# Moving the last tokens' product of blocks 2 to 5 beside the product with q, into the banks of w_res and of w_out's first product

## The chip, the cores and the metric

The kernel runs on one core of a Trainium2 chip. The metric is the device time of one execution in microseconds (us); lower is better. It is written with an order laid down by hand: nothing reorders the instructions of an engine, and each engine works through its own list in order. The engines are TensorE (PE in the profile, with its weight loads as PEld), VectorE (DVE), ScalarE (ACT), GpSimd (POOL), and the queue of SyncE (SP) for transfers.

## The reference

Attention without softmax, then a gated feed-forward part with a gated residual. Batch 8, 8 heads, 576 tokens, head size 64; so x has 4608 rows of 512, and d_ff is 1536.

```
kv  = einsum('bhsd,bhse->bhde', k, v)
out = einsum('bhsd,bhde->bhse', q, kv)
rms = sqrt(mean(out * out, axis=-1) + 1e-06)
x   = (out / rms * g_norm), heads side by side: 4608 x 512

g, val   = x @ w_gate, x @ w_val
ffn_out  = (gelu(g) * val) @ w_out
res_gate = sigmoid(x @ w_res)
result   = x + res_gate * ffn_out
```

## The kernel before, in words

**Blocks.** The first 512 tokens of batch b are block b (0 to 7). The last 64 tokens of all eight batches are gathered into block 8, two batches to a tile of 128 rows. While block m goes through the feed-forward part, the attention of batch b = m+2 is done in between. For b = 4 to 7 (blocks m = 2 to 5) this includes the last 64 tokens of a pair of batches, 2(b-4) and 2(b-4)+1, whose q lies transposed in `qrT`.

**Seven products in place of eight.** Each large product is cut in quadrants and done by Winograd's scheme with seven products of half size. A block's gate and value products run in three groups of four columns of 128 (`gv_group`, line 952). The group's order is a string of words (lines 946 to 950): `1g` is the first product of the gate, `Eg` a ScalarE copy that seeds a second PSUM bank, `Fg` and `cg` are VectorE sums, `g11` is a gelu on ScalarE, `h11` the product gelu x value. A block's last group ends `... 3g cv 3v h11 g22 4g g12 h12 4v g21 h22 h21`. Other work is hung behind a word with `at_word`, and is issued right after it.

**Banks.** PSUM has eight banks. A tile is given a bank by number, and its first writer waits until all that used the bank's former tile are done. `banks_of` (line 1522) hands a group's banks on by role. In a last group the gate's tiles A, E, F are in the banks called `ga1`, `gf`, `ge_` there, the value's in `va1`, `vf`, `ve`, and `ga0`, `va0` are free. `out_at` gives the banks of what follows, `att_at` and `pattn.opening` those of the attention's tiles.

**Behind the groups.** `res_halves` (line 577) makes the product with w_res in tiles rA, rF, rE, again by words: `1` and `6` write rA, `5` rF, `2` rE; `sE` is the ScalarE copy of rA into rE, `sd` that of rF into `rd`, `+F` the VectorE sum of rA and rd; `7` writes rA again. In blocks 2 to 5 `with_res_and_attn` (line 678) hangs attention and the first products of w_out (tiles wA, wD, wE, wF) between these words; behind `sd` it puts `a_o`, q times kv, 32 small matmuls into four tiles named op.

**The last tokens before the change.** `a_rem_kv` (line 274) takes two banks. `rem_mm` (line 282) multiplies the last tokens' q with kv: 16 matmuls of 64x64x64 for the chip's four quarters of the array, into one half of kv's own bank (kvp) and into a second bank (orp). `kv_mm` makes kv itself, 40 small matmuls, in the other half of the first bank. For b = 4 to 6 both stand behind `3g` in the block's last group; for b = 7, which needs its own kv for its last tokens, kv stands behind `5v` and `rem_mm` behind `3g`. `kv_out` (line 294) casts kv to `kv2` on ScalarE, and `rem_out` (line 297) copies the two outputs to `o32`, behind the word `g12` (for b = 7 the cast is behind `dv`). `s_begin` (line 519) is a VectorE difference of 128x1536 hidden values, hung behind `h12`.

Of the kernel before, what the change touches and what calls it, by code (L numbers as in the profile page):

```python
# [8 lines left out]
FP32 = mybir.dt.float32  # L9
# [9 lines left out]
def kernel(  # L19
# [204 lines left out]
                    )  # L224

    def a_kv(b, copy=nc.vector.tensor_copy):
        ps = pattn.tile([P, NP, D], FP32, tag="at", name="kvp")
        kv_mm(b, ps)
        copy(out=st[b]["kv2"], in_=ps)

    def a_o(b):

# [38 lines left out]
        a_sq(b, i)  # L271
        a_red(b, i)

    def a_rem_kv(b):

        kv = pattn.tile([P, 2, NP, D], FP32, tag="at", name="kvp")
        st[b]["ps"] = kv[:, 1], [kv[:, 0], pattn.tile([P, NP, D], FP32, tag="at", name="orp")]
        if 2 * pair(b) + 1 < b:
            rem_mm(b)
        kv_mm(b, kv[:, 1])  # L280

    def rem_mm(b):
        for pr in range(NP):
            for e in range(2):
                for i in range(2):
                    nc.tensor.matmul(
                        st[b]["ps"][1][e][halves(i), pr, :],
                        lhsT=st[b]["qrT"][halves(e), pr, halves(i)],
                        rhs=kv_of(2 * pair(b) + i, e, pr),
                        start=True,  # L290
                        stop=True,
                    )

    def kv_out(b):
        nc.scalar.copy(out=st[b]["kv2"], in_=st[b]["ps"][0])  # L295

    def rem_out(b):
        o32 = attnp.tile([P, C], FP32, tag="o32", bufs=3, name="o32")
        st[b]["o"][NJ] = o32
        for e in range(2):  # L300
            nc.scalar.copy(
                out=o32.rearrange("p (r e d) -> p r e d", e=2, d=D)[:, :, e, :], in_=st[b]["ps"][1][e]
            )

    def a_norm(b, j0, j1, eng=nc.vector):
# [333 lines left out]
    def out_by_products(blk, banks, amid):  # L639
# [38 lines left out]
        def with_res_and_attn():  # L678
            b = blk + 2

            def tile_of_w(n):
                w[n] = pmoe.tile([P, 2, CH], FP32, name="w" + n, bank=banks[n])

            def half_a(e):
                if e == 0:
                    tile_of_w("A")
                half("A", e, a_of(blk, 1, 1), b_of(1, 1))

            def seed():
                tile_of_w("E")  # L690
                nc.scalar.copy(out=w["E"], in_=w["A"])

            def behind_a():
                tile_of_w("F")
                tile_of_w("D")
                for e in range(2):
                    half_d(e)
                for i in (2, 3):
                    a_ss(b, i)
                w["d"] = attnp.tile([P, 2, CH], FP32, tag="sq", bufs=3, name="wd")  # L700
                nc.scalar.copy(out=w["d"], in_=w["D"])

            res_halves(blk, dict(zip("AFE", (banks[j] for j in range(3)))), {
                "sE": [lambda: sq_tile(b, 0), lambda: sq_tile(b, 1)],
                "sd": [lambda: s_sum(blk, 0), lambda: a_o(b), lambda: a_sq(b, 0), lambda: a_sq(b, 1)],
                "+F": [lambda: a_red(b, 0)],
                "2": [lambda: half_a(0)],
                "tE": [lambda: a_sq(b, NJ)],
                "+c": [lambda: s_sum(blk, 1), lambda: a_red(b, 1), lambda: a_red(b, NJ)],
                "3": [lambda: half_a(1)],  # L710
                "tF": [seed],
                "tA": [behind_a],
            }, "1 sE 5 sd 6 +F 2 tE 7 +c 3 tF 4 tA tc")
            for jj in ((0, 0), (0, 1), (1, 1), (1, 0)):
                sigmoid(jj)
# [721 lines left out]
    def plan_attn_ahead(b):  # L1437

        rem = pair(b) is not None
        m = b - 2  # L1440
        assert rem == (m in GROUPS)
        act, pool = nc.scalar.copy, nc.gpsimd
        begin = [lambda: attn_begin(b), lambda: d_qT(b)]
        if rem:
            at_word(m, 0, "h22", begin.pop(0), lambda: d_rem_qT(b))
        if m in GROUPS:
            for i in range(2):
                half = lambda i=i: by_token(b, act, slice(2 * i, 2 * i + 2))
                if whole(m):
                    at_word(m, i, "g11", half)  # L1450
                else:
                    at(m, 2 + i, half)
            if whole(m):
                at_word(m, 1, "g11", *begin)
            else:
                at(m, 3, *begin)
            if b + 1 < B:
                at(m, 2 * GF, lambda: load_behind(b))
            last = len(GROUPS[m]) - 1
        else:  # L1460
            at(m, 8, lambda: by_token(b, act, slice(0, 2)))
            at(m, 9, lambda: by_token(b, act, slice(2, 4)), *begin)
            at(m, NF, lambda: a_kv(b, act), lambda: load_behind(b, load_q))
            aside_out(m, "end", lambda: load_kv(b + 1))
        if rem:
            at_word(m + 2, 0, "cv", lambda: a_g(b, NJ, NJ + 1))
            own = 2 * pair(b) + 1 == b
            at_word(m, last, "5v" if own else "3g", lambda: a_rem_kv(b))
            at_word(m, last, "dv" if own else "g12", lambda: kv_out(b))
            if own:  # L1470
                at_word(m, last, "3g", lambda: rem_mm(b))
            at_word(m, last, "g12", lambda: rem_out(b))
        else:
            at(m, NF + 1, lambda: a_o(b), *[lambda j=j: a_ss(b, j) for j in range(NJ)])
        aside_out(m, "F", lambda: a_norm(b, 0, NJ + rem, pool))
        first = [lambda: new_block(b), lambda: a_t(b, 0), lambda: a_t(b, 1)]
        if whole(m + 1):
            aside_out(m, "01" if m + 1 == WHOLE else "11", *first[0:2])
            upper = [] if m + 1 == WHOLE else [lambda: d_xT(b, 0, 2)]
            amid_out[m].setdefault("end", [])[0:0] = [first[2], *upper]  # L1480
        else:
            at(m, NF + 3, *first)
        if whole(m + 1):
            t = [lambda j=j: a_t(b, j) for j in range(NJ)]
            if rem:
                at_word(m + 1, 0, "h21", lambda: a_t(b, NJ), lambda: d_xT(b, NJ, NJ + 1))
            first_whole = m + 1 == WHOLE
            for i, word, fs in (
                (0, "Fv", t[2:3]),
                (0, "cv", [t[3], lambda: d_xT(b, 0 if first_whole else 2, NJ)]),  # L1490
                (2 if first_whole else 1, "Fv" if first_whole else "cv", [lambda: a_g(b, 0, 2)]),
                (2, "Fv", [lambda: a_g(b, 2, NJ)]),
            ):
                at_word(m + 1, i, word, *fs)
            return
        for j in range(2, NJ + rem):
            at(m + 1, j - 2, lambda j=j: a_t(b, j))
        at(m + 1, 1, lambda: d_xT(b, 0, NJ))
        at_word(m + 1, 1, "Fv", lambda: a_g(b, 0, 2))
        at_word(m + 1, 1, "cv", lambda: a_g(b, 2, NJ))  # L1500
# [21 lines left out]
    def banks_of(blk):  # L1522
# [18 lines left out]
        if blk not in LAST:  # L1541
            if len(groups) % 2:
                ga0, ga1, va0, va1, ge_, gf, ve, vf = ga1, ga0, va1, va0, gf, ge_, vf, ve
            out_at[blk] = {0: ge_, 1: ve, 2: ga1, "A": va1, "D": ga1, "E": ve, "F": ge_}
            att_at[blk] = [gf, vf, ga0, va0]
            if res_in_halves(blk):
                out_at[blk] = {0: ga0, 1: va0, 2: ve, "A": gf, "D": vf, "E": ge_, "F": ga1}
                att_at[blk] = [ga0, va0, ve, va1]
            pmoe.turn = [out_at[blk][n] for n in "DEFA"]
        else:  # L1550
            out_at[blk] = {0: ga1, 1: va1, 2: ge_, 3: ve}
            if blk == LAST[0]:
                out_at[blk].update(A=gf, D=vf, E=ga0, F=va0)
            else:
                out_at[blk].update(A=(gf, vf), D=ga0, E=va0, F=ga1)
# [5 lines left out]
    for blk in range(B + 1):  # L1561
# [21 lines left out]
        else:  # L1583
            slots = [lambda f=f: m_gval(blk, f) for f in range(NF)]
            groups = GROUPS.get(blk, ())
            if groups:
# [1 line left out]
                slots[n:] = [None] * (NF - n)  # L1588
                ends = []
                if not res_in_halves(blk):  # L1590
                    at_word(blk, len(groups) - 1, "h12", lambda: s_begin(blk))

                def group(i, blk=blk, ends=ends):
                    if i == 0:
                        ends.extend(banks_of(blk))
                        if blk + 2 < B:
                            o = att_at[blk]
                            pattn.opening = o[2:] + o
                    order = None if i == 0 and whole(blk) else i == len(GROUPS[blk]) - 1
                    gv_group(blk, GROUPS[blk][i], ends[i], amid_gv.get((blk, i), {}), order)  # L1600

# [90 lines left out]
```

## Time and profile before

| what | time |
|---|---|
| median of 3 runs (318.71 to 319.44) | 319.14 us |
| profiled execution | 318.52 us |
| its span | 316.5 us |
| TensorE busy | 308.2 us, 97% of the span |
| VectorE busy | 275.7 us, 87% |
| ScalarE busy | 217.0 us, 69% |
| GpSimd busy | 187.4 us, 59% |

Block 2 ends at about 121 us, block 3 at 154, block 4 at 187 and block 5 at 219. In the views, a row of the timeline has start, duration, engine, line, operation, output and input, and in brackets how long the engine was idle before it and what released it. Rows of TensorE overlap: a matmul of 128x256 is issued each 0.109 us and its result is there 0.27 us after it starts, so "x4, 0.60" is 0.44 us of TensorE and then the time for the last result to arrive. ScalarE's and VectorE's rows overlap a little too; the distance from start to start is what a row costs in a queue.

### The profile page before, as it was taken

The numbers are of one execution on the slowest core, as the hardware profiler recorded it, in microseconds if no ns is written. First come the engines' busy times: TensorE is split into PE (matmuls) and PEld (weight loads), VectorE is DVE, ScalarE is ACT, GpSimd is POOL, SyncE is SP. The second block draws the span as 40 slices with busy tenths as digits, with TensorE's granted clock in tenths as the row PEclk, the third lists the DMA queues.
The fourth block names the chain that finished last, engine by engine and source line by source line (L and its number), as shares of the span: only waits on it lengthen the run. The fifth ranks groups of instructions, "written<-read, shape, count | busy, mean of one in ns | idle before, by whom it ended". The sixth has DMA issues, their size and how long they took to land.

```text
span 316.5 us, 7841 instructions
## 1 busy us (share of the span) xinstructions
PE 308.2 (97%) x3071; PEld 249.1 (79%) x3071; DVE 275.7 (87%) x489; ACT 217.0 (69%) x395; POOL 187.4 (59%) x239
## 2 busy tenths in 40 slices
PE   7899999999999999999999999999999999999993
PEld 3555756844888888888888888888888888888882
DVE  5897998989898899989998999899998777897774
ACT  4764688685958794879487948795667367736760
POOL 2883352360799579856985798408850474396332
PEclk9999999999999999999999999999999999999997
DMA  7999999899969598389936994700630003001104
GB/s 253 330 201 204 200 198 197 154 171 209 121 78 177 180 158 110 72 198 150 116 67 201 128 124 71 217 4 0 78 142 1 2 5 131 0 2 59 76 2 133
DMA packets 77398, 38.91 MB, mean 123 GB/s; under 512 B 42290, under 2 KB 75058, under 8 KB 77362
## 3 DMA queue, kind: packets, MB, share of 16 engines
q0 software_dynamic: 39296, 17.17, 43.3%
q1 hardware_dynamic: 37488, 20.71, 26.1%
q8 instruction: 24, 0.39, 0.5%
q10 hardware_dynamic: 578, 0.52, 0.5%
q14 instruction: 12, 0.10, 0.1%
HBM read 38.80 MB, written 9.44 MB: 152 GB/s over the span
## 4 chain that ended last, share of the span: by engine, by line
PE 59%; DVE 1%; issue 0%; DVEq 0%
PE Av L981 10%; PE Ag L981 10%; PE wA L549 8%; PE Fv L981 5%; PE Fg L981 5%; PE rA L600 3%; PE w L549 2%; PE Eg L981 2%; PE Ev L981 2%; PE wF L549 2%; PE wE L549 2%; PE wD L549 2%; PE rF L600 2%; PE rE L600 1%; PE kvp L218 1%; PE op L240 1%
## 5 line engine op out<-in xcount | busy, mean ns | idle before, releaser
L1018 POOL TENSOR_TENSOR hid<-ge,c 128x512 f16<-128x512 f16 x23 | 26.8, 1165 | 36.5 <-ACT ge L1012 36.5
L549 PEld LDWEIGHTS <-hid_s 128*128 128x128 f16 x384 | 37.5, 98 | 4.5
L981 PEld LDWEIGHTS <-wsv 128*128 128x128 f16 x368 | 35.6, 98 | 4.8 <-issue 0.2
L981 PEld LDWEIGHTS <-wsg 128*128 128x128 f16 x368 | 35.8, 98 | 4.2
L394 POOL TENSOR_TENSOR t<-t,g 128x512 f16<-128x512 f16 x32 | 37.8, 1210 | 0.0
L737 POOL TENSOR_TENSOR osb<-osb,t 128x512 f32<-128x512 f32 x28 | 34.0, 1244 | 0.0
L991 ACT COPY Eg<-Ag 128x512 f32<-128x512 f32 x23 | 13.4, 582 | 26.2 <-PE Ag L981 25.6
L549 PEld LDWEIGHTS <-hid 128*128 128x128 f16 x288 | 28.1, 98 | 3.3
L981 PEld LDWEIGHTS <-wg 128*128 128x128 f16 x276 | 27.0, 98 | 3.6
L981 PEld LDWEIGHTS <-wv 128*128 128x128 f16 x276 | 27.0, 98 | 3.1
L981 PE MATMUL Ag<-ts,wsg 128*128 128x256 f16 x184 | 27.6, 273 | 0.0
L981 PE MATMUL Av<-ts,wsv 128*128 128x256 f16 x184 | 27.6, 272 | 0.0
L1002 DVE TENSOR_TENSOR Fg<-Ag,d 128x512 f32<-128x512 f32 x23 | 16.0, 696 | 12.0 <-ACT d L995 9.1
L268 DVE TENSOR_REDUCE ss<-sq 128x8 f32<-128x512 f32 x32 | 20.3, 677 | 0.6 <-ACT sq L263 0.5
L549 PE MATMUL wA<-wo_ts,hid_s 128*128 128x256 f16 x168 | 20.6, 272 | 0.0
L1012 ACT ACTIVATE ge<-Eg 128x512 f16<-128x512 f32 x23 | 13.7, 597 | 9.7 <-PE Eg L981 9.7
L1012 ACT ACTIVATE ge<-c 128x512 f16<-128x512 f32 x23 | 14.4, 625 | 8.0 <-DVE c L1002 8.0
L1012 ACT ACTIVATE ge<-Fg 128x512 f16<-128x512 f32 x23 | 13.6, 591 | 8.8 <-PE Fg L981 7.0
L1002 DVE TENSOR_TENSOR c<-Ag,d 128x512 f32<-128x512 f32 x23 | 15.8, 688 | 4.2 <-PE Ag L981 4.2
L377 DVE TENSOR_TENSOR t<-op,ny 128x512 f16<-128x512 f32 x28 | 18.7, 683 | 0.9 <-POOL ny L334 0.4
L1018 DVE TENSOR_TENSOR hid<-ge,Fv 128x512 f16<-128x512 f16 x23 | 15.6, 680 | 1.5 <-ACT kv L295 1.5
L1012 ACT ACTIVATE ge<-Ag 128x512 f16<-128x512 f32 x23 | 13.7, 598 | 4.1 <-PE Ag L981 4.0
(228 smaller groups left out, 857.1 us busy)
## 6 DMA issues: line engine op xcount, KB each, us to landing
out_dram<-osb SPq DMA_DIRECT2D x14, 512.0 KB, 3.6
qraw<-in_q_dram POOLq DMA_DIRECT2D x7, 512.0 KB, 6.4
k<-in_k_dram POOLq DMA_DIRECT2D x7, 512.0 KB, 7.9
v<-in_v_dram POOLq DMA_DIRECT2D x7, 512.0 KB, 10.7
wo<-in_moe_w_out_dram POOLq DMA_DIRECT2D x3, 384.0 KB, 11.9
wg<-in_moe_w_gate_dram POOLq DMA_DIRECT2D x2, 512.0 KB, 8.4
out_dram<-osb SPq DMA_DIRECT2D x4, 256.0 KB, 5.0
wv<-in_moe_w_val_dram POOLq DMA_DIRECT2D x3, 256.0 KB, 7.5
```

The costliest lines, as they stand in the source:

```text
L218: nc.tensor.matmul(ps[halves(e), pr, :], lhsT=k16[:, h, j * D : (j + 1) * D] if j < NJ else kl[:, h, :], rhs=v16[:, h, j * D : (j + 1) * D ...
L268: nc.vector.tensor_reduce(out=out_, in_=sqs.pop((b, i)), op=ALU.add, axis=mybir.AxisListType.X)
L377: nc.vector.tensor_tensor(out=t, in0=o, in1=scale, op=ALU.mult)
L394: eng.tensor_tensor(out=t_t[blk][:, jj, :], in0=t_t[blk][:, jj, :], in1=g16, op=ALU.mult)
L549: nc.tensor.matmul(ps[:, e - es[0], :], lhsT=a[:, f, e * P : (e + 1) * P], rhs=b[:, f, :], start=(start and e == es[0] and f == 0), stop=( ...
L600: nc.tensor.matmul(out_[:, e, :], lhsT=x_[:, e, cc, :], rhs=w_[:, cc, :], start=(first and e == 0 and cc == 0), stop=(cc == 1), skip_group ...
L737: nc.gpsimd.tensor_tensor(out=res_all[of], in0=res_all[of], in1=t_t[blk][of], op=ALU.add)
L981: nc.tensor.matmul(out_[:, r, :], lhsT=lhsT, rhs=rhs, start=(first and r == 0 and c == 0), stop=(c == 1), skip_group_check=True,)
L991: nc.scalar.copy(out=tile_of("E", u), in_=ps["A", u])
L1002: nc.vector.tensor_tensor(out=dst, in0=ps["A", u], in1=sb["d", u], op=ALU.add)
L1012: nc.scalar.activation(out=ge[q], in_=source(q, "g"), func=AF.Gelu)
L1018: eng.tensor_tensor(out=dst, in0=ge[q], in1=source(q, "v"), op=ALU.mult)
```

## The change

In blocks 2 to 5 the 16 matmuls of the last tokens leave the group. They are now issued behind the first product with w_res (word `1`), followed by `a_o`, which moves there from behind `sd`, and by the two ScalarE copies, which leave `g12`. So TensorE's order is rA's first product, the 16 matmuls, op, rF; ScalarE's is the gelu of Ag, the two copies, rA to rE, rF to rd.

The 16 matmuls write two banks of their own: that of rF (the last group's Fv) and that of wA (the last group's Ag). wA and wD exchange banks, and rE goes from Ag's bank to Av's. kv has its bank alone, and takes one bank ahead of the op tiles in place of two. The VectorE difference `s_begin` moves from behind `h12` to behind `h21`, which puts it after the product of gelu with Av. Blocks 0, 1, 6, 7 and 8 have the same instructions in the same order as before, and no instruction of POOL or SP moves.

```diff
-    def a_rem_kv(b):
-        kv = pattn.tile([P, 2, NP, D], FP32, tag="at", name="kvp")
-        st[b]["ps"] = kv[:, 1], [kv[:, 0], pattn.tile([P, NP, D], FP32, tag="at", name="orp")]
-        if 2 * pair(b) + 1 < b:
-            rem_mm(b)
-        kv_mm(b, kv[:, 1])
+    def a_kv_mm(b):
+        st[b]["kvp"] = pattn.tile([P, NP, D], FP32, tag="at", name="kvp")
+        kv_mm(b, st[b]["kvp"])
+
+    def a_kv_out(b, copy=nc.scalar.copy):
+        copy(out=st[b]["kv2"], in_=st[b]["kvp"])
...
-    def rem_mm(b):
+    def a_rem(b, banks):
+        st[b]["orp"] = [pmoe.tile([P, NP, D], FP32, name="orp", bank=n) for n in banks]
         for pr in range(NP):
             for e in range(2):
                 for i in range(2):
                     nc.tensor.matmul(
-                        st[b]["ps"][1][e][halves(i), pr, :],
+                        st[b]["orp"][e][halves(i), pr, :],
...
             res_halves(blk, dict(zip("AFE", (banks[j] for j in range(3)))), {
+                "1": [lambda: a_rem(b, (banks[1], banks["A"])), lambda: a_o(b), lambda: rem_out(b)],
                 "sE": [lambda: sq_tile(b, 0), lambda: sq_tile(b, 1)],
-                "sd": [lambda: s_sum(blk, 0), lambda: a_o(b), lambda: a_sq(b, 0), lambda: a_sq(b, 1)],
+                "sd": [lambda: s_sum(blk, 0), lambda: a_sq(b, 0), lambda: a_sq(b, 1)],
...
-            at_word(m, last, "5v" if own else "3g", lambda: a_rem_kv(b))
-            at_word(m, last, "dv" if own else "g12", lambda: kv_out(b))
-            if own:
-                at_word(m, last, "3g", lambda: rem_mm(b))
-            at_word(m, last, "g12", lambda: rem_out(b))
+            at_word(m, last, "5v" if own else "3g", lambda: a_kv_mm(b))
+            at_word(m, last, "dv" if own else "g12", lambda: a_kv_out(b))
...
-            out_at[blk] = {0: ge_, 1: ve, 2: ga1, "A": va1, "D": ga1, "E": ve, "F": ge_}
+            out_at[blk] = {0: ge_, 1: ve, 2: va1, "A": ga1, "D": va1, "E": ve, "F": ge_}
...
-                    at_word(blk, len(groups) - 1, "h12", lambda: s_begin(blk))
+                    at_word(blk, len(groups) - 1, "h21", lambda: s_begin(blk))
...
-                            pattn.opening = o[2:] + o
+                            pattn.opening = o[2:3] + o
```

More of the change, by code (lines that the diff above doesn't have):

```diff
@@ L226, in a_kv @@
     def a_kv(b, copy=nc.vector.tensor_copy):
-        ps = pattn.tile([P, NP, D], FP32, tag="at", name="kvp")
-        kv_mm(b, ps)
-        copy(out=st[b]["kv2"], in_=ps)
+        a_kv_mm(b)
+        a_kv_out(b, copy)
+    def a_kv_mm(b):
[3 more added lines that the diff above has]
+        copy(out=st[b]["kv2"], in_=st[b]["kvp"])
     def a_o(b):
@@ L292, in rem_mm @@
                     )
-    def kv_out(b):
-        nc.scalar.copy(out=st[b]["kv2"], in_=st[b]["ps"][0])
     def rem_out(b):
@@ L301, in rem_out @@
             nc.scalar.copy(
-                out=o32.rearrange("p (r e d) -> p r e d", e=2, d=D)[:, :, e, :], in_=st[b]["ps"][1][e]
+                out=o32.rearrange("p (r e d) -> p r e d", e=2, d=D)[:, :, e, :], in_=st[b]["orp"][e]
             )
```

## The prediction

> **What bounds the kernel now.** I read the page's busy times first, then the table of busy time by stretch, then the timeline of block 3, and last the rows around the same place in blocks 2, 4 and 5.
>
> ```profile
> PE 308.2 (97%) x3071; PEld 249.1 (79%) x3071; DVE 275.7 (87%) x489; ACT 217.0 (69%) x395; POOL 187.4 (59%) x239
> ...
> core 0: us, PE busy (x) PEld busy (x) DVE busy (x) ACT busy (x) POOL busy (x), PEclk, DMA share, GB/s
> ...
> 186.60:219.30 32.70, 32.70 (x371) 28.60 (x369) 30.57 (x50) 24.56 (x46) 18.38 (x25) 1.00 0.34 75
> ```
>
> TensorE is the bound, and in the blocks that the change touches it is never idle: in block 5 (186.60 to 219.30) it is busy for all 32.70 us, at full clock. Between 86 and 219 us the list of waits has no wait of TensorE for another engine. So the change can't win by removing a wait of TensorE here. It can win only TensorE time, and it loses wherever it puts a wait in front of TensorE. Here is block 3 from the end of its last group into the seven products with w_res:
>
> ```profile
> 138.81 0.22 PE L286 MATMUL orp<-kv,qrT 64*64 64x64 f16 x2
> ...
> 138.93 0.20 PE L286 MATMUL orp<-kv,qrT 64*64 64x64 f16 x2
> ...
> 139.05 0.32 PE L218 MATMUL kvp<-v,k 128*64 128x64 f16 x8
> ...
> 139.81 0.61 PE L981 MATMUL Fv<-xT,wsv 128*128 128x256 f16 x4
> 139.92 0.37 ACT L295 CAST kv<-kvp 128x256 f16<-128x256 f32 x1
> ...
> 140.19 0.38 ACT L301 COPY o<-kvp 128x256 f32<-128x256 f32 x1
> 140.25 0.60 PE L981 MATMUL Ag<-ts,wg 128*128 128x256 f16 x4
> 140.45 0.39 ACT L301 COPY o<-orp 128x256 f32<-128x256 f32 x1
> 140.51 0.69 DVE L1018 TENSOR_TENSOR hid<-ge,Fv 128x512 f16<-128x512 f16 x1 [0.59 <-ACT kv L295]
> ...
> 140.89 0.60 ACT L1012 ACTIVATE ge<-Ag 128x512 f16<-128x512 f32 x1
> ...
> 141.12 0.95 DVE L512 TENSOR_TENSOR hid_s<-hid 128x1536 f16<-128x1536 f16 x1
> 141.13 0.60 PE L600 MATMUL rA<-wr,xT 128*128 128x256 f16 x4
> ...
> 141.56 0.60 PE L600 MATMUL rF<-wrs,ts 128*128 128x256 f16 x4
> 141.82 0.57 ACT L620 COPY rE<-rA 128x512 f32<-128x512 f32 x1 [0.33 <-PE rA L600]
> 141.99 0.68 DVE L1018 TENSOR_TENSOR hid<-ge,Av 128x512 f16<-128x512 f16 x1
> ...
> 142.10 0.64 PE L240 MATMUL op<-kv,qT 64*128 64x64 f16 x32
> ...
> 142.58 0.95 DVE L512 TENSOR_TENSOR hid_s<-hid 128x1536 f16<-128x1536 f16 x1
> 142.67 0.61 PE L600 MATMUL rA<-wrs,ts 128*128 128x256 f16 x4
> ...
> 143.45 0.69 DVE L627 TENSOR_TENSOR rF<-rA,rd 128x512 f32<-128x512 f32 x1
> ...
> 144.21 0.60 PE L600 MATMUL rA<-wrs,ts 128*128 128x256 f16 x4
> ```
>
> See how little is to spare. I count from the start of rA's first product, R (141.13). ScalarE copies rA into rE (141.82 to 142.39) while TensorE does rF and op, and the next product into rA (142.67, R+1.54) finds the copy done 0.28 us earlier. The seventh product (144.21, R+3.08) follows the end of VectorE's rF sum (143.45+0.69=144.14) by 0.07 us. Blocks 2 and 4 have the same offsets (R is 108.54 and 173.55, the next rA product 110.08 and 175.09).
>
> **The change, part by part, blocks 2 to 4.**
>
> *What leaves the group.* The last tokens' 16 matmuls take 0.24 us of TensorE (138.81 to 139.05, the change of array shape included). kvp and everything up to rA come 0.24 us earlier, so rA starts at R-0.24. Two ScalarE copies leave the place ahead of the gelu of Ag; kv's cast stays.
>
> *May the product start in its new place?* Its two outputs lie in the banks of Fv and Ag. The reader of Ag is that gelu: Ag's matmuls end at 140.25+0.60-0.24=140.61, the gelu starts 0.04 later (as 140.85 to 140.89 now) and ends at R+0.12. Fv's reader on VectorE starts at 140.27 and ends at R-0.17. A product of small tiles begins 0.54 after the start of the product ahead (141.56 to 142.10), thus at R+0.30. A release reaches TensorE 0.05 to 0.09 us after the releaser's end (0.07 in the rows above, 209.25 to 209.30 in block 5, 44.35 to 44.44 from the cast of batch 1's kv to its op). So there is no wait, with about 0.1 us to spare.
>
> *What is now behind it on ScalarE.* This is the step that costs. On ScalarE the order is: both copies of the result, then the copy rA to rE, then rd. Last matmul at R+0.30+0.12, its result 0.20 later (138.81, 138.93, 0.20): R+0.62. The first copy starts 0.04 (gelu row) to 0.09 later (rA ends at 141.73, the copy starts at 141.82). The next starts 0.25 to 0.27 after it (205.48 to 205.73 in block 5; 140.19 to 140.45), and rA to rE 0.25 to 0.29 after that (205.73 to 205.99; 108.02 to 108.31 in block 2): R+1.16 to R+1.27. It runs 0.57, and TensorE hears of it 0.05 to 0.09 later: R+1.78 to R+1.93. TensorE itself is ready for the second product into rA where it was before: the 0.24 us taken out in front are put in again behind rA, so R+1.54. (rF must wait for the first copy, R+1.04 to R+1.10 and 0.05 more, against R+1.11 for TensorE: 0.04 at most.) **New wait: 0.24 to 0.39 us a block; I take the middle, 0.31.** Queued behind it on TensorE is everything, as it works in order, and nothing later is idle in which the loss could be made good.
>
> *The sum of hidden rows, moved.* VectorE now does the product with Av first, then the sum. That product must await the gelu of Ag (R+0.17), where before the sum filled that time. Then 0.59 (141.99 to 142.58), two sums of 0.87 each (141.12 to 141.99, 142.58 to 143.45): the rF sum could start at R+2.50. With the second rA product at R+1.85, its result comes at R+2.46 and the rF sum at R+2.55; it ends 0.69 later and releases the seventh product at R+3.31. TensorE arrives there at R+1.85+0.44+0.44+0.66=R+3.39. So this move costs nothing, by 0.08 us; if the first wait were not there, it would itself hold the seventh product till R+3.26, 0.18 later than now.
>
> *Bank exchange (wA with wD, rE with Av).* rE must await VectorE's product with Av, R+0.85 at the latest, well before R+1.16. wA's first half runs after R+2.7 and needs the second copy, over by R+1.4. wD needs the tanh of rE, over 1 us before. Next block's banks have the same owners as before. Op's last two tiles find their banks free sooner, but op never waited. No DMA, POOL or SP instruction moves. All this: nothing.
>
> **Block 5.** Here kvp lies earlier in the group, and the 16 matmuls stand alone: taking them out gives 0.35 us (204.41 to 204.76), putting them beside op costs 0.24. Fv's reader (205.61+0.69, plus 0.05) then lets them start at 206.35, 0.09 late. Copies, rA to rE and release as above: the second rA product at 207.83 to 207.98, against 207.62. But its seventh product already waited for VectorE (rF sum 208.56 to 209.25, product at 209.30), which hides a part: 1.54 later is 209.37 to 209.52, so 0.07 to 0.22; I take 0.15.
>
> *A rule against a hoped-for gain.* Around small tiles the rows show gaps of about 0.1 us: op starts 0.10 after rF's 0.44 us, and between the last of the 16 and kvp lie 0.12. The Trainium skill (TensorEngine Tiling (Array Packing), Key Properties) says that a change of tiling mode, not only of the tile, drains TensorE. By it, 64x64 followed by op's 64x128 is a change too, so blocks 2 to 4 swap one change for another and only block 5 is rid of one, which is what I summed; if the two shapes lay together freely, up to 3 x 0.12 would go, and the sum would be 0.7 in place of 1.1.
>
> **Sum:** 3 x 0.31 + 0.15 = 1.1 us (0.8 to 1.4). The profiled execution took 318.52 us, 316.5 of span and 2.0 around it: 319.6 after, span 317.6. The median of the three runs is 319.14, 0.62 above the profiled one; with it, 320.2 us, 0.34% more. From run to run 0.2% (0.64 us) is about what can be told from no change.
>
> **Rivals.**
> 1. *The moved sum holds instead.* If ScalarE got to rA-to-rE 0.3 us sooner than I reckon, the seventh product still waits for VectorE, 0.18 us in blocks 2 to 4: +0.54, 319.7, within 0.2%. For it: VectorE's row at 143.45 is already back to back with the sum before it. Against: the copies' spacing is measured four times.
> 2. *Not slower: fewer changes of shape pay for the wait.* If op follows the 16 matmuls without a gap, 0.12 us goes in blocks 2 to 4, and 0.21 in block 5 (0.09 in front, 0.12 behind): 0.57 in all. With no wait that would be 318.6; it decides from the point where the waits of the four blocks average under 0.14 us. Against: my lowest wait is 0.24, and it hangs on ScalarE, which such gaps don't shorten.
> 3. *The product itself waits.* If the gelu of Ag starts later than 0.04 after Ag (other gelus start 0.1 after their matmuls), the margin is used up and all the rest slides with it. At 0.25 us a block more: +2.1, 321.2.
>
> **How the numbers follow.** Forecast 72% (0.8 to 1.4; with the spread of runs 319.6 to 320.9), rival 1 12%, rival 2 8%, rival 3 8%. Low end 319.2: rival 1 is in, most of rival 2 out; high end 321.2 reaches to rival 3's time. Slower: forecast and rival 3, less some 2% that fall under 0.64: 78%. Same: rival 1, those 2% and half of rival 2: 18%. Faster: 4%.
>
> **What would show it.** After the change the chain of waits should name TensorE's second rA product waiting for ScalarE's copy rE<-rA, some 0.3 us in each of blocks 2 to 4 and a little less in block 5; the idle time of TensorE between 104 and 212 us should go from near nothing to about 1.2 us; the gelu of Ag should start about 0.3 earlier; and the 16 matmuls should follow rA at its usual distance. If TensorE shows no idle there, my spacing of the three ScalarE copies is wrong; if the idle time stands ahead of the 16 matmuls, rival 3 is right; if ahead of the seventh product, rival 1.

## The result, and the profile after

The changed kernel takes 319.93 us (median of 20 executions) where the kernel before takes 319.16 us (20 executions): a ratio of 1.0024, with a 95% interval of 1.0013 to 1.0035. It is slower by 0.77 us; 1.1 were forecast. The profiled execution has a span of 317.5 us, 1.0 more than before.

The page's busy times of the changed kernel hardly differ:

```profile
PE 308.0 (97%) x3071; PEld 249.1 (78%) x3071; DVE 276.2 (87%) x489; ACT 217.1 (68%) x395; POOL 186.2 (59%) x239
```

The work is the same; the 1 us is time in which TensorE does nothing. The table by stretch shows where (length of the stretch, then the busy time of TensorE, weight loads, VectorE, ScalarE, GpSimd; last the granted clock, the DMA share and GB/s):

```profile
86.00:118.50 32.50, 32.33 (x369) 28.51 (x367) 28.65 (x48) 25.73 (x50) 25.54 (x36) 1.00 0.95 146
...
186.60:219.30 32.70, 32.56 (x370) 28.68 (x368) 30.49 (x50) 24.73 (x46) 18.25 (x25) 1.00 0.35 76
```

The same stretch at 186.60 was busy for 32.70 of 32.70 us before. TensorE now stops for the product with w_res once in each block. The waits of TensorE from 86 to 221 us, of which there was none before, are few, because most of each stop is booked on the weight loads. First TensorE's waits of the changed kernel, then, among those of its weight loads, the line of the product with w_res (the others, 0.2 us each, stand at the small tiles, as before). Both give total us, times and the longest:

```profile
PE rA L597 <- ACT rE L617: 0.2, 1, 0.2
```

```profile
PEld L597 <- issue: 1.2, 4, 0.3
```

Four stops at line 597, the product with w_res, about 0.3 us each. The timeline of block 3 shows one of them. By chance rA's first product starts at 141.13 us in both kernels, so that these rows can be laid beside those of the prediction as they are:

```profile
140.95 0.60 ACT L1010 ACTIVATE ge<-Ag 128x512 f16<-128x512 f32 x1 [0.56 <-POOL hid L1016]
...
141.13 0.60 PE L597 MATMUL rA<-wr,xT 128*128 128x256 f16 x4
...
141.58 0.69 DVE L1016 TENSOR_TENSOR hid<-ge,Av 128x512 f16<-128x512 f16 x1 [0.38 <-ACT ge L1010]
...
141.66 0.32 PE L286 MATMUL orp<-kv,qrT 64*64 64x64 f16 x16
...
141.91 0.64 PE L246 MATMUL op<-kv,qT 64*128 64x64 f16 x32
142.01 0.65 ACT L298 COPY o<-orp 128x256 f32<-128x256 f32 x2 [0.47 <-PE orp L286]
142.18 1.82 DVE L509 TENSOR_TENSOR hid_s<-hid 128x1536 f16<-128x1536 f16 x2
...
142.48 0.61 PE L597 MATMUL rF<-wrs,ts 128*128 128x256 f16 x4
...
142.55 0.61 ACT L617 COPY rE<-rA 128x512 f32<-128x512 f32 x1
...
143.20 0.60 PE L597 MATMUL rA<-wrs,ts 128*128 128x256 f16 x4
...
143.92 0.69 DVE L624 TENSOR_TENSOR rF<-rA,rd 128x512 f32<-128x512 f32 x1
...
144.07 0.82 PE L546 MATMUL wA<-wo,hid 128*128 128x256 f16 x6
...
144.73 0.60 PE L597 MATMUL rA<-wrs,ts 128*128 128x256 f16 x4
```

Follow ScalarE: the gelu at 140.95, the two copies of the last tokens' result from 142.01, and only then rA to rE at 142.55, which stood at 141.82 before. It ends at 143.16, and the second product into rA follows at 143.20. TensorE had issued rF by 142.48+0.44=142.92, so it stood still for 0.28 us. The same difference is 0.33 us in block 2 (110.58 against 110.25), 0.28 in block 4 (175.89 against 175.61) and 0.28 in block 5 (208.68 against 208.40). In block 5 the wait of 0.14 ahead of the seventh product has gone for it, so 0.13 is left there.

These sum to 0.33+0.28+0.28+0.13=1.02 us, but the kernel lost only 0.77. I cut the run from the last group of block 2 to the end of block 5 at the first Ag of block 3, 4, 5 and 6, and compared the lengths (us):

| kernel | block 2, from its last group | block 3 | block 4 | block 5 | sum |
|---|---|---|---|---|---|
| before | 20.13 | 32.58 | 32.43 | 32.66 | 117.80 |
| changed | 20.46 | 32.62 | 32.69 | 32.79 | 118.56 |
| difference | 0.33 | 0.04 | 0.26 | 0.13 | 0.76 |

Block 3 lost 0.28 at its end and still is only 0.04 longer: something gave 0.24 us back. It lies in its first group, which took 6.35 us before (121.45 to 127.80) and now takes 6.11 (121.93 to 128.04). TensorE's rows at that place in the kernel before:

```profile
122.76 0.60 PE L981 MATMUL Ag<-ts,wsg 128*128 128x256 f16 x4
123.43 0.60 PE L981 MATMUL Fv<-ts,wsv 128*128 128x256 f16 x4
```

and in the changed kernel:

```profile
123.24 0.60 PE L979 MATMUL Ag<-ts,wsg 128*128 128x256 f16 x4
123.67 0.60 PE L979 MATMUL Fv<-ts,wsv 128*128 128x256 f16 x4
```

From Ag to Fv it is 0.67 us before and 0.43 after. Four matmuls take 0.44; the kernel before had a stop of 0.24 us here, and the change removed it. It was there to be seen. The table by stretch of the kernel before has 35.33 busy of 35.40 us from 118.50 to 153.90; a row of TensorE runs on for 0.16 us after its last matmul is issued (0.60 against 0.44), so the table shows 0.07 of the 0.24 us. And the waits of weight loads of the kernel before, from 86 to 221 us, have a line for it that the changed kernel's list lacks:

```profile
PEld L981 <- issue: 0.2, 1, 0.2
```

The prediction, which looked at blocks 2 to 5 as never idle, passed it by.

### The profile page after: what moved, and what is told of

Its sections match the earlier page's. It is cut to its first block, busy times and chain, and to the rows that moved or that the text cites. A ratio compares the mean times of both kernels' runs of the same rounds, so it can differ in the third digit from the quotient of the medians.

```text
span 317.5 us, 7836 instructions
## 1 busy us (share of the span) xinstructions
PE 308.0 (97%) x3071; PEld 249.1 (78%) x3071; DVE 276.2 (87%) x489; ACT 217.1 (68%) x395; POOL 186.2 (59%) x239
## 4 chain that ended last, share of the span: by engine, by line
PE 90%; DMA 4%; DVE 2%; ACT 1%; SPq 1%; issue 0%; DVEq 0%
PE Ag L979 13%; PE Av L979 13%; PE wA L546 12%; PE Fv L979 6%; PE Fg L979 6%; PE rA L597 4%; PE gps L440 4%; PE fps L478 3%; PE vps L440 3%; PE Eg L979 3%; PE Ev L979 3%; PE wE L546 3%; PE wF L546 3%; PE wD L546 3%; PE w L546 2%; DMA qT<-q 2%
## 5 line engine op out<-in xcount | busy, mean ns | idle before, releaser
L1016 DVE TENSOR_TENSOR hid<-ge,Av 128x512 f16<-128x512 f16 x23 | 15.6, 679 | 1.1 <-ACT ge L1010 1.1
```

What stands on the lines that cost most here:

```text
L1016: eng.tensor_tensor(out=dst, in0=ge[q], in1=source(q, "v"), op=ALU.mult)
```

## The experiments

Two questions stand: is it ScalarE's order that costs the 0.3 us a block, and what took the 0.24 us away?

**1 to 4: the order on ScalarE and the moved sum, each alone and both.** All four are built on the changed kernel. In the first, ScalarE's second copy of the last tokens' result goes behind rA to rE:

```diff
...
-                "1": [lambda: a_rem(b, (banks[1], banks["A"])), lambda: a_o(b), lambda: rem_out(b)],
-                "sE": [lambda: sq_tile(b, 0), lambda: sq_tile(b, 1)],
+                "1": [lambda: a_rem(b, (banks[1], banks["A"])), lambda: a_o(b), lambda: rem_out(b, (0,))],
+                "sE": [lambda: rem_out(b, (1,)), lambda: sq_tile(b, 0), lambda: sq_tile(b, 1)],
```

> The changed kernel with one thing turned round: the second of the two copies of the last tokens' result (orp to o32) is issued behind the copy of rA into rE instead of ahead of it, in blocks 2 to 5. Theory A (ScalarE's three copies in a row hold the second product into rA, and VectorE's rF sum, 0.07 us behind, holds the seventh product next): the copy rA to rE starts at 142.32 in block 3 instead of 142.55 (the end of VectorE's product with Av, 142.27, and 0.05), so the second rA product comes about 0.23 us sooner and waits 0.05 instead of 0.28; but the rF sum stays at 143.92, as it follows the two hidden sums without a gap, and the seventh product comes at 144.66 instead of 144.73. So only 0.07 us a block, 0.3 in all: 0.15% above the kernel before, where the change stood at 0.24%. Rival B (the wait for ScalarE is the whole loss, the moved sum is hidden for good): 0.23 us a block, 0.9 in all: 0.05% below the kernel before. Rival C (the loss is elsewhere, in the banks or ahead of the product): no difference, 0.24% above.

The second leaves the order and takes the moved sum out, so that the product which reads it works on stale values:

```diff
-                    at_word(blk, len(groups) - 1, "h21", lambda: s_begin(blk))
+                    pass
```

> The changed kernel without the VectorE difference s_begin in blocks 2 to 5: the third hidden sum is left out there, so the sixth product of w_out takes stale values in these blocks. Theory A: alone this gives nothing at this place, since the second rA product waits for ScalarE as before (0.28 us) and the seventh product follows TensorE's own work; the rF sum moves up only to 143.85, where the second rA product's result is there. 0.2% to 0.24% above the kernel before; a little may come from the 0.87 us a block that VectorE is spared. Rival D (VectorE's sum is the bound, ScalarE's copies are hidden): 0.2 to 0.3 us a block, 1 us in all: at or below the kernel before.

The third does both edits:

> Both at once: the second copy behind rA to rE, and s_begin left out in blocks 2 to 5 (stale values in the sixth product of w_out there). Theory A: only now does the seventh product come sooner by as much as the second rA product does. The second rA product at 142.97 in block 3, rd's copy ends at 143.73, the rF sum starts at 143.77 and the seventh product at 144.51 instead of 144.73: 0.22 us a block, 0.9 in all, which is within 0.1% of the kernel before. More than the sum of the two alone (0.3 and 0 to 0.15). Rival B: the same as the second copy alone. Rival C: no difference from the changed kernel.

The fourth puts the sum back to where it was before the change:

```diff
-                    at_word(blk, len(groups) - 1, "h21", lambda: s_begin(blk))
+                    at_word(blk, len(groups) - 1, "h12", lambda: s_begin(blk))
```

> The changed kernel with s_begin back behind h12, ahead of VectorE's product with Av (one part of the change undone). Theory A: the product with Av then starts behind the sum at 141.99 instead of 141.58 in block 3 and ends at 142.68; rE lies in Av's bank, so the copy rA to rE starts at 142.73 instead of 142.55, the second rA product comes at 143.37, 0.17 us later, and all behind it: 0.17 us in blocks 2 to 4, less in block 5 where the product with Av comes sooner after the gelu; 0.5 to 0.7 us in all, 0.4% to 0.45% above the kernel before. Rival E (the place of the sum doesn't matter, ScalarE's queue is the later one either way): no difference, 0.24% above.

Measured, beside a median of 319.16 us for the kernel before in the same batch (30 executions), with the stretches cut as above:

| run | median, us | ratio to before, 95% | block 2, from its last group | block 3 | block 4 | block 5 |
|---|---|---|---|---|---|---|
| second copy late | 319.53 | 1.0005 (0.9990 to 1.0020) | 20.27 | 32.56 | 32.65 | 32.68 |
| sum left out | 320.24 | 1.0031 (1.0014 to 1.0048) | 20.46 | 32.62 | 32.71 | 32.79 |
| both | 319.00 | 0.9993 (0.9979 to 1.0007) | 20.18 | 32.39 | 32.47 | 32.57 |
| sum at its old place | 320.78 | 1.0045 (1.0028 to 1.0061) | 20.51 | 32.74 | 32.83 | 33.32 |

The medians have wide intervals, and the ratios are those on record, not quotients of the medians. The stretches come from one profiled execution of each kernel; in two profiles of the kernel before they agree to 0.01 us (run 6 below). With the second copy late, block 3 reads:

```profile
141.05 0.60 PE L598 MATMUL rA<-wr,xT 128*128 128x256 f16 x4
...
142.23 0.57 ACT L618 COPY rE<-rA 128x512 f32<-128x512 f32 x1
...
142.85 0.60 PE L598 MATMUL rA<-wrs,ts 128*128 128x256 f16 x4
...
143.72 0.82 PE L547 MATMUL wA<-wo,hid 128*128 128x256 f16 x6
...
143.85 0.69 DVE L625 TENSOR_TENSOR rF<-rA,rd 128x512 f32<-128x512 f32 x1
...
144.59 0.60 PE L598 MATMUL rA<-wrs,ts 128*128 128x256 f16 x4
```

The second product into rA now comes 1.80 us behind the first, 0.27 sooner than in the changed kernel, and waits for nothing. But the seventh product (144.59) is only 0.06 us nearer to rA than there (3.54 against 3.60): TensorE is ready for it at 143.72+0.66=144.38 and waits 0.21 for VectorE's rF sum, which ends at 144.54. That sum stands right behind the two sums of hidden rows. Leave the moved one out as well, and the third run has:

```profile
142.54 0.60 PE L598 MATMUL rA<-wrs,ts 128*128 128x256 f16 x4
...
143.36 0.70 DVE L625 TENSOR_TENSOR rF<-rA,rd 128x512 f32<-128x512 f32 x1 [0.61 <-ACT rd L621]
...
144.11 0.60 PE L598 MATMUL rA<-wrs,ts 128*128 128x256 f16 x4
```

VectorE is idle for 0.61 us ahead of its sum, which now follows ScalarE's rd, and the seventh product comes 3.37 us behind rA (140.74). With the sum left out alone, VectorE is idle and waits for TensorE instead, and nothing is gained:

```profile
144.42 0.70 DVE L624 TENSOR_TENSOR rF<-rA,rd 128x512 f32<-128x512 f32 x1 [0.77 <-PE rA L597]
```

So ScalarE's order is what holds, and VectorE's moved sum is 0.06 us behind it: alone, the copy wins back 0.40 us by the stretches and the sum nothing; both together win back 0.95. With the sum at its old place it stands ahead of the product of gelu with Av, whose bank rE needs, and rA to rE starts later still (143.12 with rA at 141.55, 1.57 behind where it was 1.42). TensorE's waits in that run:

```profile
PE rA L597 <- ACT rE L617: 1.3, 4, 0.6
```

The move of the sum thus belongs to the change: without it the change costs 0.84 us more. Another thing in the table was not expected. The third run loses only 0.05 in block 2 (20.18), and yet its block 3 is 0.19 shorter than before. If the stop at the start of block 3 had only been slack that a late TensorE fills, it should have been there again.

**5 and 6: the kernel before with the moved sum alone, and the kernel before once more.** The one is the edit of the fourth run the other way round, in the kernel before; the other has no edit.

```diff
-                    at_word(blk, len(groups) - 1, "h12", lambda: s_begin(blk))
+                    at_word(blk, len(groups) - 1, "h21", lambda: s_begin(blk))
```

> The kernel before with one part of the change alone: s_begin moves from behind h12 to behind h21, all else stays. By the rows of before in block 3: the gelu of Ag ends at 141.49, VectorE's product with Av then runs from 141.54 instead of 141.99, the two sums from 142.13 and 143.00, and the rF sum starts at 143.87 instead of 143.45. Theory A (VectorE's chain gelu of Ag, product with Av, two sums, rF sum is on the edge of holding the seventh product): the seventh product comes at 144.62 instead of 144.21, and the same in blocks 2, 4 and 5: 0.4 us a block, 1.4 to 1.7 us in all, 0.45% to 0.55% above the kernel before. Rival E (the sum is hidden wherever it stands): no difference.

> The kernel before once more, unchanged, for a second trace. In the first one TensorE lost 0.24 us at the start of block 3 (ahead of Fv in its first group, at 123.4), and the changed kernel did not. Theory F (that stop belongs to the kernel before: a chain through GpSimd and VectorE is late there, and part of what the change loses in block 2 is taken up by it): the stop is there again, 0.2 to 0.25 us. Rival G (chance of one execution): it isn't there.

The first takes 320.26 us, a ratio of 1.0046 (1.0034 to 1.0058). In the four blocks its seventh product waits for VectorE; its waits of TensorE from 86 to 221 us:

```profile
PE rA L600 <- DVE rF L627: 1.1, 4, 0.4
```

Counted from rA (141.42) the seventh product comes at 3.48 (144.90) against 3.08 before: about 0.4 us a block. The moved sum costs that much where TensorE is on time, and nothing behind the wait for ScalarE, as forecast. The second is one execution of 320.08 us; its opening was 1.5 us longer, and the first group of block 3 has the stop again (Ag at 124.28, Fv at 124.96). The moved-sum kernel speaks against slack too: its TensorE arrives at block 3 0.41 us later than before (20.54 against 20.13), and its first group still takes 6.35 us.

**7 to 10: can VectorE be relieved?** With the second copy late, only the moved sum is in the way. Two kernels put it on GpSimd, on top of the first run and of the kernel before, and two split it in VectorE's idle time, 1024 columns earlier in the last group and 512 at the word where the sum stood. The cuts show the edits on the changed kernel; in the kernel before, the word is `h12`:

```diff
...
-                    at_word(blk, len(groups) - 1, "h21", lambda: s_begin(blk))
+                    at_word(blk, len(groups) - 1, "1g", lambda: s_begin(blk, nc.gpsimd))
```

> The changed kernel with the second copy behind rA to rE, and with s_begin given to GpSimd ahead of the last group's words, where GpSimd stood idle for 3.3 to 4.2 us; nothing is left out. Theory A: as with both edits before, 0.22 us a block sooner than the changed kernel; GpSimd takes some 3.5 us for 1536 columns (3 x 1.17), about its idle time, so its last product of the group is at most 0.3 late, and what reads it first, the sum at 142.2, doesn't wait. 0.1% below the kernel before to 0.05% above it. Rival H (GpSimd's work slows VectorE, or its own queue with the loads comes late): 0.2% or more above the kernel before.

> The kernel before with s_begin given to GpSimd at the same place. Theory A: TensorE waited there only in block 5, 0.14 us for the rF sum, and that goes; the product with Av, bound by the gelu, comes 0.4 sooner and nothing else gains. With the 0.24 us at the start of block 3, if that goes too: 0.04% to 0.12% below the kernel before. Rival H: 0.2% or more above it.

```diff
...
-                    at_word(blk, len(groups) - 1, "h21", lambda: s_begin(blk))
+                    at_word(blk, len(groups) - 1, "Ev", lambda: s_begin(blk, 0, 4))
+                    at_word(blk, len(groups) - 1, "h21", lambda: s_begin(blk, 4, NFH))
```

> The changed kernel with the second copy behind rA to rE, and with s_begin cut in two on VectorE: the four columns of the first group (1024 values) behind the word Ev of the last group, where VectorE stood idle for 0.60 to 1.51 us ahead of Fg, the two columns of the second group (512 values) behind h21 as before. Nothing is left out. Theory A: about 0.55 us of the two sums ahead of the rF sum goes, the rF sum then starts when rd is copied (as with the sum left out), and the seventh product gains what the second rA product gained: 0.2 us a block against the changed kernel, 0.8 in all: 0.05% below to 0.05% above the kernel before. If the part put ahead of Fg makes Fg late in blocks 3 and 4 (0.60 of idle against some 0.6 of work), up to 0.1 us more there. Rival B (the order of ScalarE's copies alone decides): as with the second copy alone, 0.05% to 0.15% above.

> The kernel before with s_begin cut in two in the same way, its second part behind h12. Theory A: TensorE was never idle there but for 0.14 us ahead of the seventh product in block 5 and 0.24 us at the start of block 3. The first goes, as the rF sum moves up by some 0.5; the second hangs on GpSimd's chain for the norm, which starts from VectorE's sums of squares, and may go too: 0.04% to 0.12% below the kernel before, the fastest version if it holds.

On GpSimd the time is 322.67 us (1.0115, 1.0098 to 1.0131) and 322.04 us (1.0100, 1.0085 to 1.0115): the rival named there was right, and the loss is far more than the place of the sum had cost. The timeline of the first, in block 3's last group:

```profile
137.31 3.09 POOL L510 TENSOR_TENSOR hid_s<-hid 128x1536 f16<-128x1536 f16 x1
...
138.69 1.99 DVE L401 TENSOR_SCALAR xT<-xT,gcol 128x1024 f16<-128x1024 f16 x1
...
140.60 0.68 DVE L1001 TENSOR_TENSOR c<-Ag,d 128x512 f32<-128x512 f32 x1
```

VectorE's scaling of xT takes 0.48 us in the changed kernel (137.84). Here it takes 1.99 and ends 0.28 us after GpSimd's sum (137.31+3.09=140.40): it was held up beside that sum. The sum c behind it releases TensorE's Ag, which waited.

The split kernels take 319.59 us (1.0014, 1.0002 to 1.0027) and 319.22 us (1.0000, 0.9989 to 1.0012). In the first the list names no wait of TensorE for data from 86 to 221 us, and its stretches (20.26, 32.50, 32.52, 32.55) sum to 117.83, as before; the forecast for it, within 0.05% of the kernel before, was met by the trace and not by the median. In the second block 5 loses its old wait (32.54 against 32.66), but block 2 gets longer by 0.35; it was forecast to gain and doesn't. The trace puts it on the earlier part of the sum:

```profile
102.32 2.02 DVE L512 TENSOR_TENSOR hid_s<-hid 128x1024 f16<-128x1024 f16 x1
...
102.63 1.16 POOL L1018 TENSOR_TENSOR hid<-ge,c 128x512 f16<-128x512 f16 x1
```

It takes 2.02 us with GpSimd at work beside it, and 0.97 to 1.00 in blocks 3 to 5, where GpSimd's product ends about 0.4 us after it starts; some 0.6 had been reckoned with. VectorE's sums behind it come late, and TensorE with them.

**11 and 12: one more instruction on ScalarE.** The first group of block 3 takes 6.35 us in four kernels that have ScalarE's old order (before, its moved sum, its sum on GpSimd, its sum split) and 6.11 us in all that have the new one, whatever else they do. Walk back from the stop in the kernel before. TensorE's Fv (123.43) waits for VectorE in the trace, and starts 0.05 us after VectorE's second product of op with the norm (ny) ends (122.70+0.68=123.38):

```profile
121.49 0.69 DVE L377 TENSOR_TENSOR t<-op,ny 128x512 f16<-128x512 f32 x1 [0.40 <-POOL ny L334]
...
122.70 0.68 DVE L377 TENSOR_TENSOR t<-op,ny 128x512 f16<-128x512 f32 x1
```

VectorE works without a gap from the first of these products, and that one had waited 0.40 us for the norm on GpSimd. The norm waits for the row sums, and they for ScalarE, which is late from one instruction on. ScalarE in block 2 of the kernel before:

```profile
112.71 0.58 ACT L613 ACTIVATE th<-rF 128x512 f32<-128x512 f32 x1
113.69 0.57 ACT L691 COPY wE<-wA 128x512 f32<-128x512 f32 x1 [0.39 <-PE wA L549]
```

and of the changed kernel:

```profile
113.18 0.60 ACT L610 ACTIVATE th<-rF 128x512 f32<-128x512 f32 x1
113.89 0.57 ACT L688 COPY wE<-wA 128x512 f32<-128x512 f32 x1
```

The copy follows the start of the tanh by 0.98 us in the kernel before and by 0.71 in the changed one; in block 3 it is 0.70 and 0.71. The trace names the matmuls of wA, but their last one was issued by 113.15 (the next product starts there), and its result was there 0.17 later, at 113.32. Nothing that the trace shows holds the copy for the next 0.37 us, of which 0.09 to 0.10 is the usual distance. What differs is its place: it is ScalarE's 192nd instruction in the trace of the kernel before and the 191st in the changed one. An instruction that waits for two or more things has one ahead of it that only waits (17 ns each, 169 of them on ScalarE in the trace before and 164 after), and the change needs one fewer ahead of this place. If the stop belongs to the 192nd instruction, one more instruction in ScalarE's idle time in the opening must remove it from the kernel before and bring it into the changed one:

```diff
+    spare = consts.tile([1, 1], FP16, name="spare")
...
                 nc.scalar.preload_act_table_set("gelu_and_others")
+                nc.scalar.copy(out=spare, in_=g16[0:1, 0:1])
```

> The kernel before with one more ScalarE instruction: a copy of a single number (already made by ScalarE) in ScalarE's idle 0.58 us before the first gelu of the opening; nothing else is moved. In all four executions of the kernel before and of kernels built on it, ScalarE makes a stop of 0.28 us in block 2 right ahead of its copy wE<-wA, whose matmul was done (113.69 us in the kernel before, 7.76 us ahead of block 3, where it is 8.04 us ahead of the next block in every other block), and the norm on GpSimd and TensorE's stop of 0.24 us at the start of block 3 follow from it; in all kernels built on the change, where ScalarE has one instruction fewer ahead of that place, the copy is on time and the stop falls behind it. Theory P (the stop belongs to a place in ScalarE's stream of instructions, the change merely shifted the stream by one): with one instruction more the copy wE<-wA of block 2 is on time or the stop falls one instruction earlier, behind the tanh of rF, where the wait for the matmul covers it; the first Fv of block 3 follows Ag 0.43 to 0.44 us later and not 0.67; time 0.24 us shorter, ratio 0.9990 to 0.9995. Rival S (the stop at the start of block 3 is slack, taken up in the changed kernel by the later arrival of TensorE): nothing changes, the stop of 0.24 us stays, ratio 0.9997 to 1.0003.

> The changed kernel with the same one more ScalarE instruction in the opening. Theory P: ScalarE's copy wE<-wA in block 2 is now at the place in the stream that it has in the kernel before, so it comes 0.28 us late, 7.76 us ahead of block 3, and TensorE stops 0.24 us at the start of block 3 as in the kernel before (Fv 0.67 us behind Ag), on top of the four waits for rA to rE: 0.24 us more than the changed kernel, ratio to the kernel before 1.0028 to 1.0036 (the changed kernel 1.0024), all that the forecast had summed. Rival S (slack taken up): no stop at the start of block 3, ratio 1.0022 to 1.0026 as without the copy.

The kernel before with it takes 318.29 us where the kernel before takes 318.89: a ratio of 0.9983 (0.9961 to 1.0005). Its TensorE at the start of block 3:

```profile
122.81 0.60 PE L981 MATMUL Ag<-ts,wsg 128*128 128x256 f16 x4
123.24 0.60 PE L981 MATMUL Fv<-ts,wsv 128*128 128x256 f16 x4
```

The stop is gone, and block 3 takes 32.35 us in place of 32.58, the others 20.13, 32.44 and 32.67 as before. The changed kernel with it takes 319.96 us, 1.0033 (1.0010 to 1.0055), and the stop is there. Its copy wE<-wA of block 2 follows the start of the tanh by 0.99 us (116.62 to 117.61), where the kernel before with the spare copy has 0.69:

```profile
126.61 0.68 DVE L374 TENSOR_TENSOR t<-op,ny 128x512 f16<-128x512 f32 x1
126.68 0.60 PE L979 MATMUL Ag<-ts,wsg 128*128 128x256 f16 x4
...
127.35 0.60 PE L979 MATMUL Fv<-ts,wsv 128*128 128x256 f16 x4
```

Its block 3 takes 32.86 us, 0.24 more than the changed kernel's. The trace of the changed kernel holds the stop as well: its 192nd instruction, one that only waits, starts 0.30 us after that copy does (113.89 to 114.19), where in blocks 3 to 5 the same instruction follows within 0.03. So the 0.24 us is not due to where the last tokens' product stands: the change shifted ScalarE's stream by one instruction, and a stop that falls on a fixed place in it moved from in front of a copy to behind its start, where the copy's own 0.57 us covers it. The kernel before with the spare copy has the lowest median of all that compute the whole result; its interval reaches to 1.0005, so by the medians alone the gain isn't settled, while the trace shows it at its place.

## Why the prediction was right, point by point

- **The bound.** TensorE without a wait in blocks 2 to 5: right but for the stop of 0.24 us at the start of block 3, which was overlooked.
- **The product in its new place.** Forecast to start 0.54 us behind rA without a wait; it starts 0.53 behind (141.66), in blocks 2 to 4 alike. Rival 3, that it waits itself, is out there, though its condition came true: the gelu of Ag starts 0.10 behind Ag's result in blocks 3 to 5, not 0.04 (140.95 against 140.25+0.60 in block 3). It ends at 141.55, 0.11 ahead of the product, so little of the margin is left. For the same reason the gelu comes about 0.2 us earlier in the block and not 0.3 as the sign said: 0.18 ahead of rA, against 0.24 before, with rA 0.24 earlier.
- **ScalarE's order.** Forecast was the start of rA to rE 1.40 to 1.51 us behind rA and a new wait of 0.24 to 0.39 us, taken at 0.31. Measured: 1.42 (142.55), in block 2 1.47 (108.45 to 109.92), and waits of 0.33, 0.28 and 0.28 us in blocks 2 to 4. With the 0.28 of block 5 that is 1.17 us of idle TensorE, where the sign named 1.2. That this order is the cause was shown by the first and third run. rF, with up to 0.04 allowed for, didn't wait: it follows op by 0.57 us, the distance that the product behind op had before.
- **The moved sum.** Forecast to cost nothing, by 0.08 us, and to hold the seventh product 0.18 later if the first wait were away. Measured: VectorE's sum ends at 144.61 and would let TensorE go, at the 0.05 us that a release took in the first run, at 144.66, 0.07 ahead of where it arrives (144.73), and with the first wait away the seventh product waits 0.21. Of rival 1, that the sum holds in its place, the mechanism is real, but it needs ScalarE to be 0.3 us sooner, as the first run made it.
- **Block 5.** Forecast 0.07 to 0.22, taken at 0.15; measured 0.13. The product waits for Fv's reader, as forecast: it starts 0.64 behind rA (206.50 to 207.14), 0.11 late where 0.09 was reckoned.
- **Changes of array shape.** The two small products stand 0.25 us apart (141.66 to 141.91), as the 16 matmuls and kvp did before (0.24). The rule of the Trainium skill (TensorEngine Tiling (Array Packing), Key Properties) that a change of mode drains TensorE agrees with that, and rival 2, a gap saved, is out.
- **The sum.** The four waits gave 1.02 us where 1.1 was forecast, and the measured 0.77 lies just under the 0.8 to 1.4 that the terms add up to. The term that failed is the one for all the rest: "No DMA, POOL or SP instruction moves. All this: nothing", and with it "nothing later is idle in which the loss could be made good". It counted what instructions do and not how many there are. The true term was -0.24 us: one ScalarE instruction fewer, and a stop that no longer held block 3. 1.02-0.24=0.78, against 0.77 measured and 0.76 in the stretches. That the profile's span came out 1.0 longer, nearly as forecast, is partly luck: 0.15 of it arose before the last group of block 2 (101.32 against 101.47), in a stretch that the change leaves alone.

My first reading, that TensorE's lateness filled a slack, fell with the third and fifth run; the last two settled the matter.

## What to carry to other kernels

Before work is moved behind another product, write out the order in which its reader's engine will then serve everything, and price the instruction that lands at the end of that queue: here two copies of 0.27 us each made a third one late, and TensorE with it. When one wait is removed, look up what ends next; here, in block 3, it stood 0.06 us behind, so that neither edit alone was worth much there. And where a few tenths of a microsecond decide, compare the time of stretches that the change doesn't touch: a difference there may come from the mere position of an instruction in its stream.

## What the runs showed of the hardware

- ScalarE stops for about 0.28 us ahead of its 192nd instruction as the traces count them (113.69 in the kernel before, where 113.41 would be the usual distance from the matmul). It did so in each trace in which that instruction is the copy wE<-wA: the kernel before in two executions, the three kernels with its stream of instructions, and the changed kernel with one more. In the seven traces in which it is the waiting instruction behind that copy, it starts 0.30 us after the copy, and not 0.02 to 0.03 as in blocks 3 to 5. In the kernel before with one more, it falls where ScalarE waits for the matmul anyway, and no stop can be seen. What happens there is open; the trace shows no wait for it.
- GpSimd's sum of 128x1536 took 3.09 us where VectorE needs 0.95, and a VectorE scaling beside it took 1.99 us in place of 0.48. The Trainium skill (SBUF — State Buffer, Who interferes with whom) has a rule for this: the two engines share a pair of ports, and when a VectorE instruction runs in one of its two-port modes, whoever issues first has the pair for its whole instruction and the other stands still. The row agrees in that VectorE ends after GpSimd; that it ends only 0.28 us after, with 0.48 of work, the rule doesn't explain by itself, and no run here shows in which mode VectorE ran.
- The opening varies from one execution to the next: the last group of block 2 starts at 101.32 us in the first profile of the kernel before and at 102.84 in the second, with the same blocks behind it, and at 104.92 in that of the last run. The stretches are the better measure for a change of 0.2%.
